# Attention and FFN on one core: loads by unit in order of need, token groups of 4,2,4,4,4,4,2, and a block-diagonal state

## The chip, the cores and the metric

One core of a Trainium2 chip. The metric is the device time of one execution in microseconds (us); the span in a profile starts at the first instruction and reads about 2 us less than the time. Engines: PE (TensorE matmul), DVE (VectorE), ACT (ScalarE), POOL (GpSimd), SP (issues all DMAs here). HBM is the chip's main memory.

## The reference, cut to what matters

Linear attention with decay, then a bilinear feed-forward network (FFN). The recurrence is the kernel's own concern: it works on blocks of 128 tokens, called units here. There are 4 batches x 6 units = 24 units.

```python
# q, k, v: (4, 8, 768, 64); per head, block by block:
intra = einsum('bhic,bhjc->bhij', qb, kb) * Dmask     # decay, lower triangle
intra = einsum('bhij,bhjd->bhid', intra, vb)
inter = einsum('bhid,bhde->bhie', qb * lam_pow, kv_state)
out[block] = intra + inter
kv_state = lam_block * kv_state + einsum('bhsd,bhse->bhde', kb_dec, vb)
# x: (3072, 512) from out;   w_a, w_b: (512, 1536);   w_out: (1536, 512)
return ((x @ w_a) * (x @ w_b)) @ w_out
```

## The kernel before

Tokens go through the FFN in six groups of four units. While PE works on the FFN of one group, `hook(slot)` slips in the attention of the next group's units, in three pieces: T (transposes of q and k into `qkT`), K (k times q into `kq`, masked into `m`) and O (intra plus inter product into `o_ps`, then the update of the state). The first group's attention has no FFN to hide behind; it is the prelude. In the profiles `tps` are the transposes, `xT` is the attention's output as the FFN reads it, `a_ps` and `b_ps` are its products with w_a and w_b, `ab` is their product, and `op` is that with w_out.

```python
qr = q.rearrange("b h (nb p) d -> b p h nb d", p=BLK)
def load_batch(b, n0=0, n1=NB):                 # a whole batch in three DMAs, or single units
    ...
            if n0 == 0 and n1 == NB:
                nc.sync.dma_start(out=t[:].rearrange("p h nb d -> p (h nb) d"),
                                  in_=src[b].rearrange("p h nb d -> p (h nb) d"))
            else:
                for nb in range(n0, n1):
                    nc.sync.dma_start(out=t[:, :, nb, :], in_=src[b, :, :, nb, :])
...
def piece_O(u, xT, col):
    ...                                         # intra: 8 matmuls on 64 columns of the array
    if nb > 0:
        for hp in range(HP):
            for i in range(2):
                p = slice(64 * i, 64 * i + 64)  # inter: 8 matmuls on 64 x 64 of the array
                nc.tensor.matmul(o_ps[p, hp, :], lhsT=st[p, hp, :], rhs=qkT[p, 0, hp, :], ...)
    nc.scalar.copy(xT[:, :, col:col + BLK], o_ps)
    ...                                         # state update: 8 matmuls on 64 columns
    nc.vector.tensor_copy(st, kvd)              # 128 x 256
...
for u in range(UPG):
    prep(u, first=True)                         # vb copies on ACT
cast_w("a", 0, "dve")
cast_w("b", 0, "act")                           # before the first qkT copy in ACT's queue
load_w("b", 1); load_w("a", 2); load_batch(0, UPG, NB)
for step in range(UPG + 2):                     # prelude: T, K, O of units 0 to 3
    ...
preps = {0: 0, 3: 1, 8: 2, 12: 3}
for g in range(NG):
    def hook(slot, g=g, nxt=nxt):
        if g == 0:
            ...
            if slot == 4:
                cast_w("b", 2, "act"); load_w("o", 2)
                load_batch(1)
            ...
        if slot in preps:
            u = nxt * UPG + preps[slot]
            prep(u)
            if u % NB == NB - 1 and u // NB + 2 < B:
                load_batch(u // NB + 2)
        ...
```

Of the kernel before, what the change touches and what calls it, by code (L numbers as in the profile page):

```python
# [26 lines left out]

@with_exitstack
def kernel(
# [18 lines left out]
    N_TOK = B * S  # L48
    GT = 512
    NG = N_TOK // GT  # L50
    UPG = GT // BLK
    KS = d_model // 128
    FC = d_ff // 128
    WCH = 512
    NWC = d_ff // WCH
# [3 lines left out]
    wst_pool = ctx.enter_context(tc.tile_pool(name="wst", bufs=3))  # L59
    ld_pool = ctx.enter_context(tc.tile_pool(name="ld", bufs=2))  # L60
# [3 lines left out]
    kv_pool = ctx.enter_context(tc.tile_pool(name="kv", bufs=2))  # L64
# [13 lines left out]
    qr = q.rearrange("b h (nb p) d -> b p h nb d", p=BLK)  # L78
    kr = k.rearrange("b h (nb p) d -> b p h nb d", p=BLK)
    vr = v.rearrange("b h (nb p) d -> b p h nb d", p=BLK)  # L80
    batch_tiles = {}

    def alloc_batch(b):
        batch_tiles[b] = tuple(
            ld_pool.tile([128, H, NB, D], F32, name=n, tag=n) for n in ("qf", "kf", "vf"))

    def load_batch(b, n0=0, n1=NB):
        if b not in batch_tiles:
            alloc_batch(b)
        for t, src in zip(batch_tiles[b], (qr, kr, vr)):  # L90
            if n0 == 0 and n1 == NB:
                nc.sync.dma_start(out=t[:].rearrange("p h nb d -> p (h nb) d"),  # L92
                                  in_=src[b].rearrange("p h nb d -> p (h nb) d"))
            else:
                for nb in range(n0, n1):
                    nc.sync.dma_start(out=t[:, :, nb, :], in_=src[b, :, :, nb, :])  # L96
# [6 lines left out]
    wo_r = moe_w_out.rearrange("(ko p) n -> p ko n", p=128)  # L103
    staged = {}

    def load_w(kind, c):
        t = wst_pool.tile([128, 4, WCH], F32, name="wst", tag="wst")
        if kind == "o":
            nc.sync.dma_start(out=t, in_=wo_r[:, 4 * c:4 * c + 4, :])  # L109
        else:  # L110
            r = wa_r if kind == "a" else wb_r
            nc.sync.dma_start(out=t, in_=r[:, :, c * WCH:(c + 1) * WCH])
        staged[kind, c] = t

    def cast_w(kind, c, eng):
        t = staged.pop((kind, c))
        if kind == "o":
            dst = wo_sb[:, 4 * c:4 * c + 4, :]
        else:
            dst = (wa_sb if kind == "a" else wb_sb)[:, :, c * WCH:(c + 1) * WCH]  # L120
        if eng == "act":
            nc.scalar.copy(dst, t)
        elif eng == "dve":
            nc.vector.tensor_copy(dst, t)
        else:
            nc.gpsimd.tensor_copy(dst, t)
# [4 lines left out]
    load_batch(0, 0, UPG)  # L131
    load_w("a", 0)
    load_w("b", 0)
    load_w("a", 1)
# [12 lines left out]
                            base=0, pattern=[[1, 128]], channel_multiplier=-1)  # L147
    tmpe = singles.tile([128, NB, H], F32, name="tmpe")
# [6 lines left out]
    lotri_bc = _bc(lotri, [lotri.ap[0], [0, HP], lotri.ap[1]])  # L155


    U = {}
    kv_state = {}

    def prep(u, first=False):
        b, nb = divmod(u, NB)
        qf, kf, vf = batch_tiles[b]
        qs = prep_pool.tile([128, H, D], BF16, name="qs", tag="qs")
        ks = prep_pool.tile([128, H, D], BF16, name="ks", tag="ks")
        vb = prep_pool.tile([128, H, D], BF16, name="vb", tag="vb")
        lq = lp_q[:, nb].to_broadcast([128, H, D])
        lk = lp_k[:, nb].to_broadcast([128, H, D])
        (nc.vector if first else nc.gpsimd).tensor_mul(qs, qf[:, :, nb, :], lq)  # L169
        nc.gpsimd.tensor_mul(ks, kf[:, :, nb, :], lk)  # L170
        if first:
            nc.scalar.copy(vb, vf[:, :, nb, :])
        else:
            nc.vector.tensor_copy(vb, vf[:, :, nb, :])  # L174
        U[u] = dict(qs=qs, ks=ks, vb=vb)

    def piece_T(u):
        d = U[u]
        tps = ps_bank("tps", [128, 2, HP, 128], BF16)
        for j, src in enumerate((d["qs"], d["ks"])):  # L180
            for hp in range(HP):
                nc.tensor.transpose(tps[:, j, hp, :], src[:, 2 * hp:2 * hp + 2, :], ident)  # L182
        qkT = qkT_pool.tile([128, 2, HP, 128], BF16, name="qkT", tag="qkT")
        nc.scalar.copy(qkT, tps)  # L184
        d["qkT"] = qkT

    def piece_KQ(u):
# [14 lines left out]
    def piece_O(u, xT, col):  # L202
        b, nb = divmod(u, NB)
        d = U.pop(u)
        ks, vb, qkT, m = d["ks"], d["vb"], d["qkT"], d["m"]
        o_ps = ps_bank("o_ps", [128, HP, 128], F32)
        for hp in range(HP):
            for i in range(2):
                p = slice(64 * i, 64 * i + 64)
                nc.tensor.matmul(o_ps[p, hp, :], lhsT=vb[:, 2 * hp + i, :], rhs=m[i][:, hp, :],  # L210
                                 start=(hp == 0), stop=(nb == 0), skip_group_check=True)
        if nb > 0:
            st = kv_state[b]
            for hp in range(HP):
                for i in range(2):
                    p = slice(64 * i, 64 * i + 64)
                    nc.tensor.matmul(o_ps[p, hp, :], lhsT=st[p, hp, :], rhs=qkT[p, 0, hp, :],  # L217
                                     start=False, stop=True, skip_group_check=True)
        nc.scalar.copy(xT[:, :, col:col + BLK], o_ps)  # L219
        if nb < NB - 1:  # L220
            if nb == 0:
                kv_state["ps"] = kvps_pool.tile([128, HP, D], F32, name="kvd", tag="kvd")
            kvd = kv_state["ps"]
            for hp in range(HP):
                for i in range(2):
                    p = slice(64 * i, 64 * i + 64)
                    nc.tensor.matmul(kvd[p, hp, :], lhsT=ks[:, 2 * hp + i, :], rhs=vb[:, 2 * hp + i, :],  # L227
                                     start=(nb == 0 and hp == 0), stop=True, skip_group_check=True)
            st = kv_pool.tile([128, HP, D], BF16, name="st", tag="st")
            nc.vector.tensor_copy(st, kvd)  # L230
            kv_state[b] = st
# [4 lines left out]
    def ffn(g, xT, hook):  # L236
        ab = ab_pool.tile([128, FC, GT], BF16, name="ab", tag="ab")
        for f in range(FC):
            fsl = slice(f * 128, (f + 1) * 128)
            a_ps = ps_bank("a_ps", [128, GT], F32)  # L240
            for s in range(KS):
                nc.tensor.matmul(a_ps, lhsT=wa_sb[:, s, fsl], rhs=xT[:, s, :],  # L242
                                 start=(s == 0), stop=(s == KS - 1))
            a_sb = a_pool.tile([128, GT], BF16, name="a_sb", tag="a")
            nc.scalar.copy(a_sb, a_ps)  # L245
            b_ps = ps_bank("b_ps", [128, GT], F32)
            for s in range(KS):
                nc.tensor.matmul(b_ps, lhsT=wb_sb[:, s, fsl], rhs=xT[:, s, :],  # L248
                                 start=(s == 0), stop=(s == KS - 1))
            nc.vector.tensor_mul(ab[:, f, :], a_sb, b_ps)  # L250
            hook(f)
        for t in range(UPG):
# [8 lines left out]
            nc.sync.dma_start(out=out_r[g * UPG + t], in_=o_sb)  # L261
# [5 lines left out]
    def new_xT(g):  # L267
        xTs[g] = xT_pool.tile([128, KS, GT], BF16, name="xT", tag="xT")

    new_xT(0)  # L270
    for u in range(UPG):
        prep(u, first=True)
    cast_w("a", 0, "dve")
    cast_w("b", 0, "act")
    load_w("b", 1)
    load_w("a", 2)
    load_batch(0, UPG, NB)
    for step in range(UPG + 2):
        if step < UPG:
            piece_T(step)  # L280
        if 0 <= step - 1 < UPG:
            piece_KQ(step - 1)
        if 0 <= step - 2 < UPG:
            piece_O(step - 2, xTs[0], (step - 2) * BLK)


    plan = {}
    base = [0, 4, 9, 14]
    offs = [(1, 2, 4), (1, 2, 4), (1, 2, 3), (1, 2, 3)]
    for kk in range(UPG):  # L290
        for name, o in zip("TKO", offs[kk]):
            plan.setdefault(base[kk] + o, []).append((name, kk))
    preps = {0: 0, 3: 1, 8: 2, 12: 3}

    for g in range(NG):
        nxt = g + 1
        if nxt < NG:
            new_xT(nxt)

        def hook(slot, g=g, nxt=nxt):  # L300
            if g == 0:
                if slot == 0:
                    cast_w("a", 1, "dve")
                    load_w("b", 2)
                if slot == 1:
                    cast_w("b", 1, "act")
                    load_w("o", 0)
                if slot == 3:
                    cast_w("a", 2, "dve")
                    load_w("o", 1)  # L310
                if slot == 4:
                    cast_w("b", 2, "act")
                    load_w("o", 2)
                    load_batch(1)
                if slot == 7:
                    cast_w("o", 0, "pool")
                if slot == 9:
                    cast_w("o", 1, "pool")
                if slot == 10:
                    cast_w("o", 2, "pool")  # L320
            if nxt >= NG:
                return
            if slot in preps:
                u = nxt * UPG + preps[slot]
                prep(u)
                if u % NB == NB - 1 and u // NB + 2 < B:
                    load_batch(u // NB + 2)
            for name, kk in plan.get(slot, ()):
                u = nxt * UPG + kk
                if name == "T":  # L330
                    piece_T(u)
                elif name == "K":
                    piece_KQ(u)
                else:
                    piece_O(u, xTs[nxt], kk * BLK)

        ffn(g, xTs[g], hook)
        del xTs[g]
# [30 lines left out]
```

## Time and profile before

| | before |
|---|---|
| time, median of 3 | 306.51 us (304.59 to 306.56) |
| span of the profiled run | 304.6 us, granted clock 0.938 |
| PE busy | 238.3 us, 78% |
| HBM read and written | 28.32 and 6.29 MB |

The page's span in 40 slices of 7.6 us: busy tenths of PE, the clock that PE was granted, busy tenths of the DMA engines, and GB/s.

```profile
PE   0205899600007699999999999999999999999995
PEclk9999999955557799999999999999999999999999
DMA  7999969999997016930910001100011000110002
GB/s 146 218 337 387 219 221 290 218 218 277 217 218 138 37 69 157 220 75 22 253 72 0 2 0 74 67 3 0 2 69 69 3 0 2 69 71 0 0 34 103
```

Slices are counted from 0. From slice 14 on PE is full. Before it there are two losses: a slow start, and a hole in slices 8 to 11 in which PE stands, its clock is halved, and the DMA engines are busy throughout. Note the two rates: about 218 GB/s and, in slice 3 (23 to 30 us), 387.

The timeline of the start, columns: start us, us, engine, line, operation, in square brackets the idle time before it and what ended it.

```profile
23.49 1.90 ACT L122 CAST wb_sb<-wst 128x2048 bf16<-128x2048 f32 x1 [4.80 <-DMA wst<-in_moe_w_b_dram]
25.29 1.92 ACT L184 COPY qkT<-tps 128x1024 bf16<-128x1024 bf16 x2
...
35.08 1.02 PE L242 MATMUL a_ps<-xT,wa_sb 128*128 128x512 bf16 x4 [0.43 <-ACT xT L219]
```

ACT takes its queue in order. The first `qkT` copy stands behind the cast of w_b, which waits for its data; the FFN begins at 35.08 us.

The timeline of the hole: first SP's whole-batch loads, then what stopped and what moved again.

```profile
45.98 0.82 SPq L92 DMA_DIRECT2D qf<-in_q_dram  x1
47.25 8.94 SPq L92 DMA_DIRECT2D kf<-in_k_dram  x1
56.64 6.74 SPq L92 DMA_DIRECT2D vf<-in_v_dram  x1
...
70.77 0.70 SPq L92 DMA_DIRECT2D qf<-in_q_dram  x1
...
83.39 1.04 POOL L169 TENSOR_TENSOR qs<-qf,lp_q 128x512 bf16<-128x512 f32 x1 [33.85 <-DMA qf<-in_q_dram]
84.48 0.61 PE L182 MATMUL tps<-ident,qs 128*128 128x128 bf16 x4 [26.24 <-POOL qs L169]
90.62 1.04 POOL L170 TENSOR_TENSOR ks<-kf,lp_k 128x512 bf16<-128x512 f32 x1 [6.20 <-DMA kf<-in_k_dram]
91.72 0.61 PE L182 MATMUL tps<-ident,ks 128*128 128x128 bf16 x4 [6.63 <-POOL ks L170]
97.47 1.15 DVE L174 CAST vb<-vf 128x512 bf16<-128x512 f32 x1 [42.68 <-DMA vf<-in_v_dram]
```

PE waits for the q of unit 6, the first unit of batch 1, until 84.48 us, then for its k and, through `m`, for its v. The three tensors' first readers start at 83.39, 90.62 and 97.47 us, about 7.0 us apart: 1.57 MB each at about 223 GB/s.

The O piece of one unit between FFN matmuls, in PE's timeline:

```profile
123.45 1.03 PE L248 MATMUL b_ps<-xT,wb_sb 128*128 128x512 bf16 x4
124.41 0.41 PE L210 MATMUL o_ps<-m,vb 128*64 128x128 bf16 x8
124.75 0.41 PE L217 MATMUL o_ps<-qkT,st 64*64 64x128 bf16 x8
125.09 0.32 PE L227 MATMUL kvd<-vb,ks 128*64 128x64 bf16 x8
125.34 1.04 PE L242 MATMUL a_ps<-xT,wa_sb 128*128 128x512 bf16 x4
```

Four FFN matmuls take 0.86 us (the step from one a_ps line to the next b_ps line in a dense stretch), so the b_ps group is over at 124.31, and the O piece with its changes of tile costs 125.34 - 124.31 = 1.03 us.

### The profile page before, as it was taken

The numbers are of one execution on the slowest core, as the hardware profiler recorded it, in microseconds if no ns is written. First come the engines' busy times: TensorE is split into PE (matmuls) and PEld (weight loads), VectorE is DVE, ScalarE is ACT, GpSimd is POOL, SyncE is SP. The second block draws the span as 40 slices with busy tenths as digits, with TensorE's granted clock in tenths as the row PEclk, the third lists the DMA queues.
The fourth block names the chain that finished last, engine by engine and source line by source line (L and its number), as shares of the span: only waits on it lengthen the run. The fifth ranks groups of instructions, "written<-read, shape, count | busy, mean of one in ns | idle before, by whom it ended". The sixth has DMA issues, their size and how long they took to land.

```text
span 304.6 us, 4308 instructions
## 1 busy us (share of the span) xinstructions
PE 238.3 (78%) x1760; PEld 116.0 (38%) x1760; DVE 102.6 (34%) x168; ACT 103.3 (34%) x156; POOL 53.5 (18%) x56
## 2 busy tenths in 40 slices
PE   0205899600007699999999999999999999999995
PEld 0104544200002254444444444454454444444442
DVE  2113695000002523464125542264512554213410
ACT  4027475200002134533344334434344343333321
POOL 1500332000019621212212121212211000000000
PEclk9999999955557799999999999999999999999999
DMA  7999969999997016930910001100011000110002
GB/s 146 218 337 387 219 221 290 218 218 277 217 218 138 37 69 157 220 75 22 253 72 0 2 0 74 67 3 0 2 69 69 3 0 2 69 71 0 0 34 103
DMA packets 41059, 34.87 MB, mean 114 GB/s; under 512 B 19536, under 2 KB 33360, under 8 KB 41040
## 3 DMA queue, kind: packets, MB, share of 16 engines
q1 hardware_dynamic: 41040, 34.61, 46.1%
q8 instruction: 13, 0.21, 0.3%
q14 instruction: 6, 0.05, 0.1%
HBM read 28.32 MB, written 6.29 MB: 114 GB/s over the span
## 4 chain that ended last, share of the span: by engine, by line
PE 66%; SPq 16%; DMA 8%; DVE 5%; issue 2%; ACT 2%; DVEq 0%; ACTq 0%
PE op L255 19%; PE a_ps L242 18%; PE b_ps L248 17%; SPq L92 9%; DMA vf<-in_v_dram 5%; SPq L96 4%; PE tps L182 3%; DVE m L199 3%; DMA wst<-in_moe_w_b_dram 3%; PE o_ps L210 2%; SPq L109 2%; PE kq L194 2%; PE o_ps L217 2%; PE kvd L227 1%; DVE ab L250 1%
## 5 line engine op out<-in xcount | busy, mean ns | idle before, releaser
L250 DVE TENSOR_TENSOR ab<-a_sb,b_ps 128x512 bf16<-128x512 bf16 x72 | 49.3, 687 | 86.0 <-PE b_ps L248 85.8
L242 PE MATMUL a_ps<-xT,wa_sb 128*128 128x512 bf16 x288 | 75.0, 383 | 0.4 <-ACT xT L219 0.4
L248 PE MATMUL b_ps<-xT,wb_sb 128*128 128x512 bf16 x288 | 74.8, 383 | 0.0
L255 PE MATMUL op<-wo_sb,ab 128*128 128x512 bf16 x288 | 68.3, 387 | 0.0
L245 ACT CAST a_sb<-a_ps 128x512 bf16<-128x512 f32 x72 | 42.2, 587 | 58.3 <-PE a_ps L242 58.3
L199 DVE TENSOR_TENSOR m<-kq,lotri 128x512 bf16<-128x512 f32 x48 | 30.8, 683 | 35.2 <-PE kq L194 35.1
L248 PEld LDWEIGHTS <-wb_sb 128*128 128x128 bf16 x288 | 28.4, 98 | 34.6 <-issue 1.1
L184 ACT COPY qkT<-tps 128x1024 bf16<-128x1024 bf16 x24 | 24.2, 1013 | 45.1 <-PE tps L182 45.1
L169 POOL TENSOR_TENSOR qs<-qf,lp_q 128x512 bf16<-128x512 f32 x20 | 20.8, 1041 | 102.1 <-PE tps L182 49.7
L255 PEld LDWEIGHTS <-ab 128*128 128x128 bf16 x288 | 26.7, 99 | 30.9 <-issue 2.3
L170 POOL TENSOR_TENSOR ks<-kf,lp_k 128x512 bf16<-128x512 f32 x24 | 26.3, 1098 | 65.9 <-PE kvd L227 39.3
L242 PEld LDWEIGHTS <-wa_sb 128*128 128x128 bf16 x288 | 26.1, 98 | 27.9 <-issue 1.0
L182 PE MATMUL tps<-ident,qs 128*128 128x128 bf16 x96 | 10.4, 238 | 32.6 <-POOL qs L169 26.2
L260 ACT COPY o_sb<-op 128x512 f32<-128x512 f32 x24 | 14.0, 585 | 46.8 <-PE op L255 46.8
L174 DVE CAST vb<-vf 128x512 bf16<-128x512 f32 x20 | 10.8, 540 | 42.7 <-DMA vf<-in_v_dram 42.7
L219 ACT CAST xT<-o_ps 128x512 bf16<-128x512 f32 x24 | 14.0, 585 | 30.1 <-PE o_ps L217 18.7
L182 PEld LDWEIGHTS <-qs 128*128 128x128 bf16 x96 | 7.7, 106 | 37.8 <-POOL qs L169 26.7
L194 PE MATMUL kq<-qkT 64*128 64x128 bf16 x192 | 10.3, 231 | 14.0 <-ACT qkT L184 14.0
L182 PE MATMUL tps<-ident,ks 128*128 128x128 bf16 x96 | 10.4, 238 | 10.8 <-POOL ks L170 10.7
L210 PE MATMUL o_ps<-m,vb 128*64 128x128 bf16 x192 | 11.6, 230 | 4.8 <-DVE m L199 4.2
L194 PEld LDWEIGHTS <-qkT 64*128 64x128 bf16 x192 | 5.8, 99 | 23.6 <-ACT qkT L184 16.8
L210 PEld LDWEIGHTS <-vb 128*64 128x64 bf16 x192 | 7.0, 112 | 14.7 <-issue 8.4
(26 smaller groups left out, 65.3 us busy)
## 6 DMA issues: line engine op xcount, KB each, us to landing
out_dram<-o_sb SPq DMA_DIRECT2D x24, 256.0 KB, 2.0
wst<-in_moe_w_a_dram SPq DMA_DIRECT2D x3, 1024.0 KB, 6.5
wst<-in_moe_w_b_dram SPq DMA_DIRECT2D x3, 1024.0 KB, 6.9
wst<-in_moe_w_out_dram SPq DMA_DIRECT2D x3, 1024.0 KB, 7.3
qf<-in_q_dram SPq DMA_DIRECT2D x6, 256.0 KB, 4.9
kf<-in_k_dram SPq DMA_DIRECT2D x6, 256.0 KB, 5.1
vf<-in_v_dram SPq DMA_DIRECT2D x6, 256.0 KB, 5.1
qf<-in_q_dram SPq DMA_DIRECT2D x3, 0.2 KB, 12.5
```

Of the source, the lines that this page charges most:

```text
L92: nc.sync.dma_start(out=t[:].rearrange("p h nb d -> p (h nb) d"), in_=src[b].rearrange("p h nb d -> p (h nb) d"))
L170: nc.gpsimd.tensor_mul(ks, kf[:, :, nb, :], lk)
L182: nc.tensor.transpose(tps[:, j, hp, :], src[:, 2 * hp:2 * hp + 2, :], ident)
L184: nc.scalar.copy(qkT, tps)
L194: nc.tensor.matmul(kq[i][:, hp, :], lhsT=qkT[p, 1, hp, :], rhs=qkT[p, 0, hp, :], start=True, stop=True, skip_group_check=True)
L199: nc.vector.tensor_mul(m, kq[i], lotri_bc)
L210: nc.tensor.matmul(o_ps[p, hp, :], lhsT=vb[:, 2 * hp + i, :], rhs=m[i][:, hp, :], start=(hp == 0), stop=(nb == 0), skip_group_check=True)
L242: nc.tensor.matmul(a_ps, lhsT=wa_sb[:, s, fsl], rhs=xT[:, s, :], start=(s == 0), stop=(s == KS - 1))
L245: nc.scalar.copy(a_sb, a_ps)
L248: nc.tensor.matmul(b_ps, lhsT=wb_sb[:, s, fsl], rhs=xT[:, s, :], start=(s == 0), stop=(s == KS - 1))
L250: nc.vector.tensor_mul(ab[:, f, :], a_sb, b_ps)
L255: nc.tensor.matmul(op, lhsT=ab[:, f, t * 128:(t + 1) * 128], rhs=wo_sb[:, f, :], start=(f == 0), stop=(f == FC - 1))
```

## The change

It has three intents: load what is needed first, unit by unit, with weights in smaller chunks; let a group of two units follow the first, so that the second group needs less data early; and do inter product and state update as full 128 x 128 matmuls, on a state that is kept block-diagonal (two heads per tile, zeros between them). The core of the diff:

```diff
+GROUPS = (4, 2, 4, 4, 4, 4, 2)
+W_CHUNKS = (256, 256, 512, 512)
+LOOKAHEAD = 6
-    def load_batch(b, n0=0, n1=NB):
-        ...
+    def load_unit(u):
+        b, nb = divmod(u, NB)
+        for n, src in (("qf", qr), ("kf", kr), ("vf", vr)):
+            t = ld_pool.tile([128, H, D], F32, name=n, tag=n)
+            nc.sync.dma_start(out=t, in_=src[b, nb])
@@ piece_O
+        if nb > 0:
+            for hp in range(HP):
+                nc.tensor.matmul(o_ps[:, hp, :], lhsT=kv["st"][:, hp, :], rhs=qkT[:, 0, hp, :], ...)
-        (8 intra, then 8 inter matmuls per unit)
+        (the same 8 intra matmuls)
-                    nc.tensor.matmul(kvd[p, hp, :], lhsT=ks[:, 2 * hp + i, :], rhs=vb[:, 2 * hp + i, :], ...)
-            nc.vector.tensor_copy(st, kvd)
+                nc.tensor.matmul(kv["ps"][:, hp, :], lhsT=qk[:, 1, 2 * hp:2 * hp + 2, :],
+                                 rhs=vb[:, 2 * hp:2 * hp + 2, :], ...)
+            nc.vector.tensor_mul(st, kv["ps"], bdiag_bc)
@@ prelude
-    cast_w("a", 0, "dve")
-    cast_w("b", 0, "act")
-    load_w("b", 1)
-    load_w("a", 2)
-    load_batch(0, UPG, NB)
     for step in range(n0 + 2):
         ...
+        if step == 2:
+            cast_w("a", 0, "dve")
+            cast_w("b", 0, "act")
+            load_w("a", 3)
+            load_w("b", 3)
@@ hook
-                    load_batch(1)
-                if u % NB == NB - 1 and u // NB + 2 < B:
-                    load_batch(u // NB + 2)
+                    prefetch(n0 + LOOKAHEAD)
+                prefetch(u + 1 + LOOKAHEAD)
(cut: mask for the block-diagonal state, slot plan by group size, six staging buffers for weights, q and k in one tile, FFN of n units)
```

## The prediction

> **What bounds it now.** By windows, from 136 to 256 us PE is busy 39.86 of every 40 us; from 60 to 96 us only 4.9 of 36 at a granted clock of 0.53. The timeline shows PE stopped from 57.6 to about 92 us and limping until 102 us. Three parts:
>
> 1. Start, 35.1 us to the first a_ps matmul. ACT runs in order: the cast of wb_sb stands before the first qkT copy and ends at 25.4 us, its data late; the four-unit attention prelude then takes 9.7 us.
> 2. Steady matrix work. A token group of four units costs 38.6 us (starts at 115.0, 153.8, 192.5, 230.9, 269.8); the last, which carries no attention for a next group, 31.1. So FFN is 6 x 31.1 = 187 us and attention 1.9 us per unit, 20 units = 38 us.
> 3. The hole: 304.6 - 35.1 - 187 - 38 - 3.7 (tail after the last matmul) = about 41 us. DMA share is 0.96 to 1.10 up to 97 us; the second group needs two units of batch 1, but whole batches are loaded, and batch 2 is queued before those are used.
>
> **DMA rates.** Heads' rows are 256 B: a unit's tensor (256 KB) takes 1.14 to 1.18 us in the chain, 222 GB/s; weights in 2 KB rows 2.7 us per MB, 388 GB/s. The Trainium skill, "DMA: Bandwidth & Descriptors", section Specifications, puts line rate at 512 B and more; this trace agrees. The change keeps the 256 B rows, so no byte gets cheaper. Only the order changes.
>
> **After, worked out.** Units 0 to 3 have landed at 18 us as before; ACT frees at about 18.7, and qkT starts there instead of at 25.3. The prelude takes 9.7 us plus two half-size casts and the longer state copies (128x512 instead of 128x256, estimated 0.69 against 0.42 us): first a_ps at about 30 us, saving 5. Remaining weights land at about 43 us; units 4 and 5 at 47 and 50 us, needed only after 55; units 6 to 9 at 54 to 64 us, needed from about 66. The hole closes: 41 us.
>
> **Matmuls.** The inter product loses four of eight matmuls (0.34 us for the eight, 4 x 56 = 0.22 for the new four, by the transposes' rate), kv update 0.25 to 0.22. "TensorEngine Tiling (Array Packing)", Key Properties, says that changing the mode drains the array; the trace shows the first a_ps group after a tiled piece at 0.97 us instead of 0.86. So 0.1 us per unit, 2 us in all. Groups of 256 tokens double the number of matmuls per column, hidden (128-column transposes run at 56 ns with their loads).
>
> **New losses.** The first two group boundaries end on an attention piece whose xT copy the next a_ps waits for, about 1 us each; in the first two-unit group four attention units stand in 16 us of FFN, so DVE and ACT latencies show: 2 to 3 us.
>
> Sum: 30 + 187 + 20 x 1.8 + 4 + 3.7 = 261 us span; runs read 2 us more: 263 us.
>
> **Right or wrong in the profile:** PE filled from 30 us, granted clock full after the prelude, no wait of PE or DVE for vf or qf after 30 us. Group periods of 38 us.
>
> **What would spoil it:** loads still late (unit 6 after 66 us); PE waiting in the two-unit group by over 5 us; steady groups slower because the inter product now waits for the state.
>
> Chances: faster 0.97, same 0.02, slower 0.01.

## The result and the profile after

The time fell from 306.53 us (median of 4, 304.59 to 306.82) to 259.02 us (median of 4, 258.70 to 259.38). The ratio is 0.845, with a 95% interval of 0.840 to 0.850. Here and below, a ratio is the mean time of one kernel's runs over the mean of the other's in the same rounds, so it is not quite the ratio of the medians. The predicted time was 263, with a range of 255 to 273.

The same four lines of the page of the changed kernel (span 257.0 us, slices of 6.4 us):

```profile
PE   0308799999899999999999999999999999999994
PEclk9999999999999999999999999999999999999998
DMA  6999999999999998016397017300002200012102
GB/s 130 219 253 362 385 386 311 204 212 220 227 262 200 221 257 162 7 43 136 111 212 155 5 40 160 112 15 0 4 0 82 84 0 0 3 40 82 43 1 82
```

The hole is gone, and the clock stays full. DMA is just as busy in its first 100 us and moves the units no faster (221 GB/s from 50 to 90 us): the same bytes, in another order.

The start in the timeline:

```profile
18.62 1.92 ACT L215 COPY qkT<-tps 128x1024 bf16<-128x1024 bf16 x2
...
22.89 1.05 ACT L141 CAST wb_sb<-wst 128x1024 bf16<-128x1024 f32 x1
...
29.45 1.02 PE L269 MATMUL a_ps<-xT,wa_sb 128*128 128x512 bf16 x4 [0.35 <-ACT xT L247]
```

All waits of PE in the whole run, longest first (us in total, times, longest):

```profile
PE kq L225 <- ACT qkT L215: 8.4, 2, 8.1
PE tps L213 <- DVE qk L193: 7.6, 2, 6.3
PE o_ps L240 <- DVE st L256: 1.7, 2, 0.9
PE tps L213 <- POOL qk L194: 1.6, 2, 1.0
PE a_ps L269 <- ACT xT L247: 1.4, 3, 0.7
PE a_ps L269 <- DVE wa_sb L143: 0.7, 2, 0.4
```

The first four lie in the prelude, but for 0.23 us of the first. After 30 us there remain the group boundaries (xT) and two casts: about 2 us. From 29.4 us on, neither PE nor DVE waits for a load of q, k or v; only POOL does (5.0 us in all), and PE never waits for POOL there.

The O piece, as above:

```profile
97.90 1.03 PE L275 MATMUL b_ps<-xT,wb_sb 128*128 128x512 bf16 x4
98.76 0.39 PE L240 MATMUL o_ps<-qkT,st 128*128 128x128 bf16 x4
99.08 0.41 PE L245 MATMUL o_ps<-m,vb 128*64 128x128 bf16 x8
99.43 0.40 PE L252 MATMUL kvd<-vb,qk 128*128 128x128 bf16 x4
99.66 1.03 PE L269 MATMUL a_ps<-xT,wa_sb 128*128 128x512 bf16 x4
```

It now costs 99.66 - 98.76 = 0.90 us instead of 1.03.

From the first a_ps of each group in PE's timeline, a balance of the spans. The last column is the time from the last group's start to the end.

| kernel | first a_ps | groups, us from start to start | last |
|---|---|---|---|
| before | 35.08 | 79.72, 38.88, 38.66, 38.42, 38.88 | 35.0 |
| after | 29.45 | 36.16, 23.64, 37.75, 37.98, 37.97, 34.42 | 19.6 |

### The profile page after: what moved, and what is told of

It is laid out like the page before. It is cut to its first block, busy times and chain, and to the rows that moved or that the text cites. A ratio compares the mean times of both kernels' runs of the same rounds, so it can differ in the third digit from the quotient of the medians.

```text
span 257.0 us, 4297 instructions
## 1 busy us (share of the span) xinstructions
PE 232.0 (90%) x1696; PEld 124.8 (49%) x1696; DVE 107.2 (42%) x181; ACT 104.8 (41%) x169; POOL 52.5 (20%) x59
## 4 chain that ended last, share of the span: by engine, by line
PE 85%; SPq 5%; DVE 4%; ACT 2%; DMA 2%; issue 1%; DVEq 0%
PE a_ps L269 24%; PE op L282 24%; PE b_ps L275 24%; SPq L109 4%; PE tps L213 4%; PE kq L225 3%; PE o_ps L245 3%; DMA vf<-in_v_dram 2%; PE kvd L252 2%; DVE m L230 2%; PE o_ps L240 1%; DVE wa_sb L143 1%; ACT o_sb L287 1%; ACT xT L247 1%; DVE ab L277 1%
## 5 line engine op out<-in xcount | busy, mean ns | idle before, releaser
L277 DVE TENSOR_TENSOR ab<-a_sb,b_ps 128x512 bf16<-128x512 bf16 (+1 forms) x84 | 51.2, 611 | 89.4 <-PE b_ps L275 75.9
L269 PE MATMUL a_ps<-xT,wa_sb 128*128 128x512 bf16 (+1 forms) x336 | 76.1, 349 | 2.0 <-ACT xT L247 1.4
L275 PE MATMUL b_ps<-xT,wb_sb 128*128 128x512 bf16 (+1 forms) x336 | 76.0, 349 | 0.0
L272 ACT CAST a_sb<-a_ps 128x512 bf16<-128x512 f32 (+1 forms) x84 | 44.1, 525 | 58.4 <-PE a_ps L269 58.3
L275 PEld LDWEIGHTS <-wb_sb 128*128 128x128 bf16 x336 | 32.9, 98 | 29.4
L193 POOL TENSOR_TENSOR qk<-qf,lp_q 128x512 bf16<-128x512 f32 x20 | 20.8, 1042 | 97.9 <-issue 83.8
L194 POOL TENSOR_TENSOR qk<-kf,lp_k 128x512 bf16<-128x512 f32 x24 | 25.0, 1042 | 12.6 <-DMA kf<-in_k_dram 12.5
L213 PE MATMUL tps<-ident,qk 128*128 128x128 bf16 x192 | 16.6, 233 | 9.1 <-DVE qk L193 7.6
L213 PEld LDWEIGHTS <-qk 128*128 128x128 bf16 x192 | 13.5, 104 | 13.9 <-DVE qk L193 7.8
L256 DVE TENSOR_TENSOR st<-kvd,bdiag 128x512 bf16<-128x512 f32 x20 | 13.8, 690 | 11.7 <-PE kvd L252 11.3
L240 PE MATMUL o_ps<-qkT,st 128*128 128x128 bf16 x80 | 7.8, 219 | 1.7 <-DVE st L256 1.7
```

What stands on the lines that cost most here:

```text
L193: (nc.vector if first else nc.gpsimd).tensor_mul(qk[:, 0], qf, lq)
L194: nc.gpsimd.tensor_mul(qk[:, 1], kf, lk)
L213: nc.tensor.transpose(tps[:, j, hp, :], d["qk"][:, j, 2 * hp:2 * hp + 2, :], ident)
L269: nc.tensor.matmul(a_ps[:, :gt], lhsT=wa_sb[:, s, fsl], rhs=xT[:, s, :gt], start=(s == 0), stop=(s == KS - 1))
L272: nc.scalar.copy(a_sb[:, :gt], a_ps[:, :gt])
L275: nc.tensor.matmul(b_ps[:, :gt], lhsT=wb_sb[:, s, fsl], rhs=xT[:, s, :gt], start=(s == 0), stop=(s == KS - 1))
```

## The experiments

There were eleven runs, ten edited kernels and the changed kernel once more; all gave correct results. Labels in b start from the kernel before, those in a from the changed kernel. In each section the median of the kernel before is that of the same rounds.

### Which batch was queued first

The compiled program's issue order on SP, with the buffer numbers kept, and the first reader of batch 1 on POOL, showed something that I had read past (this is a listing of the program, not a view of the profile):

```
23 L92 DMACopy qf_482<-in_q_dram 128x48x64 [waits DMAHW3_49]
26 L109 DMACopy wst_502<-in_moe_w_out_dram 128x4x512 [waits DMAHW6_49,DMAHW0_49,Activation_49]
27 L92 DMACopy qf_504<-in_q_dram 128x48x64 [waits DMAHW7_49,Pool_49]
21 L169 TensorTensor qs_616<-qf_504,lp_q_135 128x512 [waits DMAHW7_49,DVE_49]
```

Unit 6 reads the load that was issued second. `prep(5)` runs at slot 3 and calls `load_batch(2)`; `load_batch(1)` stands at slot 4. So batch 2 goes ahead of batch 1. The experiment swaps them.

```diff
-                    load_batch(1)
+                    load_batch(2)
...
-                    load_batch(u // NB + 2)
+                    load_batch(1 if u == NB - 1 else u // NB + 2)
```

> The kernel before with one thing changed: the two whole-batch loads queued in the first group change places, batch 1 (which the second group needs) ahead of batch 2 (which nothing needs for another 80 us). Bytes, shapes and all compute are as before. Theory A, the hole of the kernel before is a matter of the order of loads: the third tensor of batch 1 lands one batch earlier, 3 x 7.1 us = 21 us (plus the 2.7 us of the last w_out chunk that stands between them), so the time falls by 21 to 24 us, to about 283. Rival B, the hole is one of bandwidth, all the bytes asked for in the first 97 us are needed: no gain.

Measured: 281.42 us against 307.29, ratio 0.916 (0.912 to 0.919). PE's and DVE's waits for unit 6 in the timeline:

```profile
61.31 0.40 PE L182 MATMUL tps<-ident,qs 128*128 128x128 bf16 x4 [1.83 <-POOL qs L169]
...
68.55 0.61 PE L182 MATMUL tps<-ident,ks 128*128 128x128 bf16 x4 [6.84 <-POOL ks L170]
...
74.35 0.43 DVE L174 CAST vb<-vf 128x512 bf16<-128x512 f32 x1 [18.32 <-DMA vf<-in_v_dram]
```

The v of unit 6 is there at 74.35 instead of 97.47 us, 23.1 us earlier. The time fell by 25.9 us, a little more than the 21 to 24 expected; the first group took 54.46 us instead of 79.72. Over half of the hole was two lines in the wrong order, not bandwidth: rival B falls. What is left is that whole batches come tensor by tensor, so a unit waits for the end of all three.

### The loads alone

The kernel before with `load_unit` and six unit buffers; units 4 and 5 are loaded ahead of the later weights as before, then 6, 7, 8 and so on. Groups of four, the old matmuls.

```diff
-    load_batch(0, UPG, NB)
+    load_unit(4)
+    load_unit(5)
...
-                    load_batch(1)
+                    for u in range(6, 12):
+                        load_unit(u)
...
-                if u % NB == NB - 1 and u // NB + 2 < B:
-                    load_batch(u // NB + 2)
+                if u >= 6 and u + 6 < B * NB:
+                    load_unit(u + 6)
```

> The kernel before with the loading part of the change alone: every unit loaded for itself, units in order of need, 6 in flight; groups of four units, order of casts, matmul tiles and slot plan as before. Theory A: nearly the whole hole of 41 us closes; what stays is 2 to 3 us, because units 6 and 7 land at about 58 and 62 us and the first is wanted at 57.6. Time about 268 us. Rival C, the grouping 4,2,4,4,4,4,2 is what lets the loads catch up: with groups of four much of the hole stays, time above 280 us.

Measured: 266.89 us against 307.29, ratio 0.868 (0.865 to 0.871); span 264.8. The first two groups start at:

```profile
34.98 1.02 PE L237 MATMUL a_ps<-xT,wa_sb 128*128 128x512 bf16 x4 [0.43 <-ACT xT L214]
...
75.06 1.03 PE L237 MATMUL a_ps<-xT,wa_sb 128*128 128x512 bf16 x4
```

So the first group takes 40.08 us instead of 79.72, and the later groups are the same to 0.01 us (38.88, 38.66, 38.42, 38.88). All of PE's waits for transposes and O pieces in that run, which are mostly the prelude's:

```profile
PE tps L177 <- DVE qs L164: 7.6, 2, 6.2
PE tps L177 <- POOL ks L165: 1.4, 2, 1.0
PE o_ps L205 <- DVE m L194: 1.4, 3, 0.6
```

Loading by unit in order of need gives by itself 304.6 - 264.8 = 39.8 us of the 47.6 by which the span fell, and it does so with groups of four. Rival C falls. How much of this is the order of units and how much the smaller loads was not tested apart, beyond the swap above.

### The matmuls alone

The kernel before with the block-diagonal state (the `piece_O` part of the diff above and the mask), nothing else.

> The kernel before with the matmul part of the change alone: inter product and kv update as full-array matmuls on a block-diagonal state. In the trace of the changed kernel the O piece of a unit takes 0.90 us between the FFN matmuls around it, before 1.03. Only what comes after the hole counts, about 17 units: 2 us, time about 304.5 us (ratio 0.993). If the tiles' mode changes cost more than I read, up to 5 us.

Measured: 305.75 us against 307.29, ratio 0.9955 (0.992 to 0.999). After the hole every group takes 38.1 us (38.11, 38.11, 38.11, 38.10) instead of 38.4 to 38.9: over these four 2.4 us, as expected. Not all of it is the form of the matmuls. The edit also puts the inter product, which needs no `m`, ahead of the intra product. In the kernel before, PE waits for `m` inside the O piece of each group's third unit, which stands only half a w_out tile after its K piece:

```profile
180.05 0.77 PE L210 MATMUL o_ps<-m,vb 128*64 128x128 bf16 x8
180.75 0.41 PE L217 MATMUL o_ps<-qkT,st 64*64 64x128 bf16 x8
```

These eight matmuls take 0.70 us there, 0.47 in this run, and 0.35 where nothing is late: the order gives 0.23 of the 0.6 us per group. The run as a whole gained less than the 2.4 us, because the first a_ps came at 36.58 instead of 35.08 us and the hole ended about 2 us later (first transpose of unit 6 at 86.62 instead of 84.48). The later start lies in the prelude: the first `qkT` copy came no later (25.18 us against 25.29), but the state copies take 0.69 instead of 0.42 us, and PE waits for them twice, 1.2 us in all, which it didn't before.

### The early casts alone

The kernel before with the two casts and the loads behind them moved after step 2 of the prelude, as in the diff.

> The kernel before with the start part of the change alone: the first two weight casts come after the third step of the attention prelude, so ACT is not held up by the weights and the first FFN matmul comes about 5 us earlier. Theory A: the hole after it ends when the loads end, whatever the start: the hole grows by what the start saves and the time stays within 1 us of before. Rival D, savings at the start are worth their length anywhere: 5 us less, about 301 us.

Measured: 306.25 us against 307.29, ratio 0.996 (0.993 to 1.000). The first a_ps came at 29.78 us, 5.3 earlier. But the timeline of PE reads:

```profile
57.25 1.03 PE L248 MATMUL b_ps<-xT,wb_sb 128*128 128x512 bf16 x4
83.56 0.61 PE L182 MATMUL tps<-ident,qs 128*128 128x128 bf16 x4 [25.28 <-POOL qs L169]
90.82 0.61 PE L182 MATMUL tps<-ident,ks 128*128 128x128 bf16 x4 [6.66 <-POOL ks L170]
```

The last FFN matmuls before the hole start at 57.25 us, before at 57.22: the lead was gone even before the hole. PE had waited 2.9 us for unit 4 at 35 us, and then worked for a while at half rate (a b_ps group of 1.91 us instead of 1.03). (The granted clock of 38.8 to 40.8 us was 0.50.) The q and k of unit 6 came 0.9 us earlier than before, but the w_out matmuls after the hole ran slower (18 of them in 6.65 us instead of 5.75), and the second group began at 115.09 us, before at 114.80. So the profiled run kept nothing of the 5.3 us, and the medians differ by 1 us, at the edge of the interval. Theory A holds, rival D falls: the loads set the pace, and time saved ahead of them is worth next to nothing.

### The same two parts undone in the changed kernel

First the matmuls: `piece_O` with 64-wide tiles as before, in the changed kernel.

> The changed kernel with the matmul part undone: inter product and kv update as 64-wide tiles again, eight matmuls each. By the traces of both kernels the O piece is 0.13 us longer, times 20 units that have both: 2.6 us slower, 261.6 us. If the block-diagonal form is worth nothing, as its longer state copy (128x512) on DVE eats it: 259.

Measured: 261.36 us, ratio to the kernel before 0.850 (0.847 to 0.852), against 259.02 for the changed kernel. The second to sixth groups are 0.54, 0.31, 0.54, 0.34 and 0.25 us longer, together 2.0 us for 18 units (0.11 each; 0.13 for each of 20 was expected). The time of 261.6 us that was expected came out partly by luck: the rest of the span's 2.7 us is not the tiles', as the start was 0.9 us earlier, and the first group 1.6 us longer, of which 1.3 us is a weight cast on DVE that took 2.64 instead of 1.36 us (more on this below).

Then the casts: the two before the prelude's steps again.

```diff
+    cast_w("a", 0, "dve")
+    cast_w("b", 0, "act")
+    load_w("a", 3)
+    load_w("b", 3)
     for step in range(n0 + 2):
...
-        if step == 2:
-            (the same four lines)
```

> The changed kernel with the start part undone: the first two casts stand before the attention prelude again, and ACT waits for the first chunk of w_b. That chunk is only half a megabyte now and lands at about 21 us: the first qkT copy starts at about 22 instead of 18.7 us, the casts in the middle of the prelude (1.7 us) go away. Theory A: with the hole closed, PE is busy from the first FFN matmul to the end, so the start counts in full: 1.5 to 3 us slower, about 261 us. If there were still slack behind it: 259.

Measured: 262.30 us, ratio to before 0.853 (0.851 to 0.856). The first a_ps moved from 29.45 to 33.45 us, more than expected (4.0 instead of at most 3), and the span from 257.0 to 260.9. The groups are the same to within 0.2 us. The casts come before the first `qkT` copy again, which starts at 22.07 us instead of 18.62. The medians differ by 3.3 us, of different rounds. So the same edit that was worth about 1 us in the kernel before is worth its whole length here, 3 to 4 us.

### Groups of four in the changed kernel

```diff
-GROUPS = (4, 2, 4, 4, 4, 4, 2)
+GROUPS = (4, 4, 4, 4, 4, 4)
...
                     load_w("o", 0)
                     load_w("o", 1)
+                    prefetch(n0 + LOOKAHEAD)
...
                     load_w("o", 2)
-                    prefetch(n0 + LOOKAHEAD)
```

> The changed kernel with groups of 4,4,4,4,4,4, and the units 4 to 9 loaded before the last w_out chunk. Unit 4 is then wanted at about 33 us, at the second slot of the first group, and lands at about 43. Theory: PE stands for about 10 us there, the two boundaries that end on an attention piece (about 1 us each) go away: 266 to 269 us. If the grouping of 4,2 is not what gives the loads time: 259 or less.

Measured: 274.25 us, ratio to before 0.892 (0.889 to 0.895); 5 us worse than I expected. PE waited 10.9 us for unit 4, as expected, but also 4.2 us for the last w_out chunk. My edit had put that chunk behind 18 loads of unit tensors (six units), so this run does not measure the grouping cleanly. The next one does it better.

### Loads, casts and matmuls together, on groups of four

The kernel with loads by unit, plus the early casts, plus the block-diagonal state; groups, slots, weight chunks and staging buffers as before.

> The kernel before with three parts of the change together, loads by unit, early casts and the block-diagonal state, but still groups of four, weight chunks of 512 columns, three staging buffers and the old slot plan. What it lacks against the changed kernel is the grouping 4,2,... with its slots. Alone, the loads gave a span of 264.8; the start is 5.3 us earlier and the matmuls 2.2 us shorter, but with groups of four the first group wants unit 4 at once and should wait some 3 us for it, as it did where the casts alone were moved. Theory E, the parts add up and the grouping buys that wait: span about 260.5, time 262.5. Rival F, the grouping buys nothing: time 259 or less.

Measured: 263.41 us against 306.74, ratio 0.858 (0.856 to 0.861); the changed kernel, run again in the same rounds, 259.12. The first a_ps came at 30.09 us, 4.9 earlier than with the loads alone, but the first group took 44.05 us, 4.0 longer. PE's timeline has the reason:

```profile
36.38 0.61 PE L182 MATMUL tps<-ident,qs 128*128 128x128 bf16 x4 [2.68 <-POOL qs L169]
37.53 0.61 PE L182 MATMUL tps<-ident,ks 128*128 128x128 bf16 x4 [0.54 <-POOL ks L170]
```

With groups of four the second group's first unit is wanted two FFN steps after the start, and waiting for it leaves PE at half rate behind it. The early start is given back there: 3.2 us of waiting, and one a_ps group at half rate (granted clock 0.54 from 37 to 40 us). Theory E holds against rival F: on groups of four the early start is lost, in the changed kernel it is not. That the two-unit group is what keeps it, as it lets unit 4 come after the weights, is likely (with groups of four the changed kernel waits for unit 4 too, 10.9 us above), but the last step below holds other edits as well. The chain of spans:

| kernel | span |
|---|---|
| before | 304.6 |
| + loads by unit, in order of need | 264.8 |
| + early casts, block-diagonal state | 261.5 |
| + groups 4,2,..., slot plan, chunks and staging buffers: the change | 257.4 (run again) |

The last step, 4.1 us, was not taken apart by a run. An estimate from the group times: the first group of this run is 44.05 - 38.11 = 5.9 us longer than its later ones, and the changed kernel loses 2.9 us in its first two groups (worked out below), so about 3 us is the waiting at the start of the FFN and about 1 us the slot plan.

### A better version

In the changed kernel the prelude still begins when everything has landed: unit 0 is there at 7.4 us, but its `qkT` copy stands in ACT's queue behind the `vb` copies of all four units, the last of which waits for its data until 18.1. The next two runs issue each unit's preparation in its own step, and give the first weight casts to POOL, which is idle then.

```diff
-    for u in range(n0):
-        prep(u, first=True)
     for step in range(n0 + 2):
         if step < n0:
-            piece_T(step)
+            prep(step, first=True)
         (K of step - 1, O of step - 2)
-        if step == 2:
-            cast_w("a", 0, "dve")
-            cast_w("b", 0, "act")
+        if step < n0:
+            piece_T(step)
+        if step == n0 - 1:
+            cast_w("a", 0, "pool")
+            cast_w("b", 0, "pool")
```

> An attempt at a better version: the changed kernel with the attention prelude pipelined with the loads. Each unit's preparation is issued in its own step, so ACT copies qkT of unit 0 when it is there and not after v of unit 3, and the first two casts go to POOL, idle then. Units land every 3.6 us; after unit 3 (18.1 us) only its own chain is left: first a_ps at about 23 us instead of 29.5. Theory A, the start counts in full: about 6 us faster, 253 us; less, if the weights (last w_b chunk at about 35 us) then hold up the first group.

Measured: 256.62 us, ratio to before 0.835 (0.833 to 0.838); less than hoped. The first a_ps came at 25.08 us, not 23, at half rate, and the timeline of the first group has this:

```profile
39.16 1.89 POOL L145 CAST wo_sb<-wst 128x2048 bf16<-128x2048 f32 x1 [17.04 <-DMA wst<-in_moe_w_out_dram]
...
39.21 2.92 DVE L143 CAST wa_sb<-wst 128x2048 bf16<-128x2048 f32 x1
...
42.19 1.04 PE L269 MATMUL a_ps<-xT,wa_sb 128*128 128x512 bf16 x4 [1.97 <-DVE wa_sb L143]
```

A DVE cast of that size takes 1.22 us where POOL does nothing (36.07 us in the changed kernel's second run). The Trainium skill, "SBUF — State Buffer", section Who interferes with whom, says that a DVE copy or cast can use a port pair that it shares with GpSimd, and that whichever comes second is blocked for the first one's whole instruction. The trace agrees: POOL's cast ends at 41.05 us, and DVE's at 42.13, 1.08 us after it. In the run with 64-wide tiles above (POOL's cast from 41.62 to 43.52, DVE's from 41.95 to 44.59) it is the same, 1.07 us after, and so it is in the changed kernel, where the two overlap by only 0.3 us (1.09 us after).

The second version moves the casts of the last w_a and w_b chunks one slot earlier, away from POOL's, gives two more casts to POOL in the prelude, and puts O ahead of K in each step, so that the state is ready for the last O piece.

> The pipelined prelude, mended where its first run lost: the state update of a unit goes ahead of the next unit's K piece (the last O piece waited 1.0 us for it), the first four half-size weight casts all go to POOL, and the casts of the last w_a and w_b chunks come one slot earlier, ahead of POOL's first w_out cast, beside which the DVE cast took 2.92 us instead of 1.22 and held PE up by 2.0 us. Expected: 3 us off the pipelined version's 256.6, about 253.5 us. If the DVE cast is slow for another reason than POOL working beside it (it should then stay at 2 us or more): about 255.5.

Measured: 253.90 us (253.85 to 254.26) against 259.12 (259.06 to 259.18) for the changed kernel and 306.74 for the kernel before in the same rounds; ratios to the latter 0.827 (0.825 to 0.830) and 0.844 (0.842 to 0.847). So this version beats both, the changed kernel by 5.2 us, or 2.0% by the ratio of the two ratios. The first a_ps came at 23.48 us, and the cast is short again:

```profile
36.92 1.22 DVE L143 CAST wa_sb<-wst 128x2048 bf16<-128x2048 f32 x1
```

The first group still lost 1.2 us against the changed kernel's (37.35 against 36.16); its first b_ps group took 1.91 us, half rate (why is not shown: the profile gives a clock of 1.00 for that stretch).

The changed kernel was run again beside it, with this expectation, which held (first a_ps at 30.02):

> The changed kernel itself, once more, beside the two below on the same chip, so that they can be compared with it. 259 us, and a first a_ps within 1 us of 29.45.

## Why the prediction was right

The time lay inside the range, 4 us below the middle. Point by point:

- **The hole of 41 us closes.** Right in size: the loads alone took 39.8 us off the span.
- **Why there was a hole.** Half wrong. The prediction says "whole batches are loaded, and batch 2 is queued before those are used". It took batch 2 as coming behind batch 1 and did not see that it goes ahead of it. Swapping the two alone brought unit 6's v 23.1 us forward. The issue order with its buffer numbers would have told this before any run; the profile's names leave buffer numbers out.
- **The start, 30 instead of 35 us.** Right (29.45). That it counts in full was assumed in the sum; the runs show that it does in the changed kernel (3 to 4 us when undone) and doesn't where the loads set the pace (1 us alone).
- **Matmuls, 0.1 us per unit.** Right: 0.13 us in the two traces' O pieces, 2.0 us for 18 units when undone. In the old slot plan the edit gave 0.15 (38.7 - 38.1 us per four units), as it also shortened the wait for `m`.
- **Attention at 1.8 us per unit.** Mis-sized: from the groups of four, (37.9 - 31.1) / 4 = 1.70. I had taken off the matmuls' 0.1 us from 1.9 and nothing for waits of the old slot plan: before, the O piece of a group's third unit came only half a w_out tile after its K piece and waited 0.35 us for `m` (0.70 instead of 0.35 us, above), 0.09 us per unit. That is 20 x 0.1 = 2.0 us of the 4. The new slots and the new order inside the O piece overlap in this: with the old slots and the new matmuls a unit costs (38.11 - 31.1) / 4 = 1.75, with the new slots and the old matmuls (38.3 - 31.1) / 4 = 1.80.
- **New losses of 4 us.** Mis-sized: the first group is 36.16 - 31.1 - 2 x 1.70 = 1.7 us over its work, the second 23.64 - 15.6 - 4 x 1.70 = 1.2. Together 2.9. The earlier start (0.55) and rounding make up the rest.
- **What would spoil it**: none came. PE's waits for the state are in the prelude alone.

## What to carry to other kernels

When DMA is busy all through a stretch in which PE waits, ask first whether the bytes in flight are those that the waiting instruction needs; check the issue order by buffer, since a load called from two places can go out the wrong way round. A saving is worth something only where the next wait is not set by another resource: the same two casts gave about 1 us while loads set the pace and 3 to 4 us after. Once the loads are in order, look at what in-order queues hold back: a copy whose data is there can stand behind one whose data is not.

## What the Trainium skill lacked or had wrong

- "TensorE: Matmul & The Clock Gate", Back-to-back issue gap: it gives about 131 ns per matmul of 512 columns and 81 ns per matmul of 128 columns as the sustained rate of pairs of weight load and matmul. Here 24 such pairs with 512 columns took 5.18 us in the chain of the changed kernel, 216 ns each, and 8 transposes of 128 columns 0.45 us, 56 ns each. The isolated gap of the same section (N / 2.4 + 2.5, so 216 and 56 ns) is what this kernel sustains.
- "TensorEngine Tiling (Array Packing)", Key Properties: it says that a change of mode drains the array and gives no size. Here a group of tiled matmuls after full-array ones starts 0.10 us late (124.41 instead of 124.31), and in the changed kernel the full-array O matmuls start with no gap (98.76). That the 0.10 us is the drain and nothing else is not shown.
- "DMA: Bandwidth & Descriptors", Why small descriptors are slow: it names an overhead of 27% for 256-byte descriptors on an internal bus, and 32 bytes of descriptor metadata for each operation, but the page has no rate for such loads from HBM on trn2. Here loads of 256-byte rows ran at 218 GB/s, loads of 2-KB rows at 386: 44% less.
- "SBUF — State Buffer", Who interferes with whom: it was right, and gives no size for a DVE cast beside a POOL cast. Here a DVE cast of 128x2048 took 2.92 and 2.64 us beside a POOL cast instead of 1.22.
